# Loading q in 1 KB pieces, four tokens to a partition, in a fused retention and ELU feed-forward kernel

## The chip, the cores and the metric

The kernel runs on one core of one Trainium2 chip. The metric is the device time of one execution in microseconds (us); lower is better. A run of the kernel before stands for the median of three timed runs; the profile is of one further execution.

## The reference, cut to what matters

```python
# q, k, v: (8, 8, 576, 64) float32: batch B, heads H, tokens S, head size D
scores = (1 / sqrt(D)) * q @ k.T                  # per batch and head
gamma  = 1 - 2.0 ** (-5 - arange(H))
Dmat   = where(rel >= 0, gamma ** rel, 0)         # rel = query token - key token
ret    = (scores * Dmat) @ v
x      = ret.transpose(0, 2, 1, 3).reshape(4608, 512)
h      = x @ w_in                                 # w_in: (512, 2048)
g      = where(h > 0, h, exp(min(h, 0)) - 1)
out    = g @ w_out                                # w_out: (2048, 512)
```

The first half is causal retention with one decay for each head, the second a feed-forward layer with an ELU between its two products. Nothing is normalised over a row, so the causal part can be split into blocks with a running state between them.

## The kernel before, in words

**Units.** The first 512 tokens of each batch are cut into four units, 32 in all (`seq`, NS = 32). For the first three batches (units 0 to 11) a unit is 256 tokens (T is 0 or 1) of four heads (w is 0 or 1). From batch 3 on the units are "fine": 128 tokens of all eight heads. The last 64 tokens of each batch are "riders" that are taken along later. The change touches units 0 to 11 alone, and the riders only in the name of a table.

**A unit's steps.** `load(u)` issues three DMAs of 256 KB from SP: q and k into the two halves of the tile rqk, v into rv. In units 0 to 11 a partition holds two neighbouring tokens (e is 0 or 1) of four heads, so the DMA moves pieces of 2 tokens x 64 x 4 bytes = 512 bytes, 128 partitions x 4 heads = 512 pieces to a load. `cast_qk` multiplies q by its decay table gq, k by gk, and rounds to bf16 into the tile qkn, in one instruction for each e; the engine is named by the caller (VectorE "v" or GpSimd "p"). `cast_v` rounds v into vn. `turn_pe` turns q and k on TensorE with eight transposes into PSUM and two copies into qkT (units 0 to 6); `turn` does the same with a transposing DMA from SP (unit 7 on). `scores` makes key x query blocks in the PSUM tile sc, `masks` multiplies by the causal mask into pt, `inter` adds what the running state gives, `values` multiplies pt by v, and `put_x` copies the result to xt, which is x transposed. `state`, `prefix_mid` and `prefix_end` update the running state (mid, end), whose bf16 copies on GpSimd go to s_pair and s_last.

**Feed-forward.** `ffn1` and `ffn1_half` multiply xt by w_in, the ELU runs on ScalarE (exp, relu) and VectorE (one combination), and `ffn2` multiplies by w_out. The weights come as 32 DMAs of 256 KB in 2 KB pieces (`load_w`) and are rounded to bf16 by `cast_w`.

**Order.** Each engine keeps the order in which the program issues (`pin`). By hand it is: loads of units 0 to 3 (unit 3 with v first, then k, then q), twelve weight loads, then units 0 to 3 as they arrive; then the feed-forward of batch 0 beside the remaining weights; the loads of unit 4, four more weight loads, and units 5 to 9 follow on SP. `turn_pe(4)`, `stretch(4)`, `turn_pe(5)`, `stretch(5)` and so on sit between quarters of `ffn2` (`quad`). Unit 7's transposing DMA follows the loads of unit 9 on SP. From there on `stage` mixes feed-forward jobs with one `step` per unit.

**DMA completion.** In the built program every DMA from SP takes the next of eight completion semaphores in turn and waits, before it is issued, for the DMA eight places earlier. The tile rqk has ten buffers, which units and weight loads share.

Of the kernel before, what the change touches and what calls it, by code (L numbers as in the profile page):

```python
# [17 lines left out]
def kernel(  # L18
# [23 lines left out]
    MID = S // 2  # L42
    C = 64
# [3 lines left out]
    const = ctx.enter_context(tc.tile_pool(name="const", bufs=1))  # L47
# [15 lines left out]
    pin = tc.keep_in_program_order  # L63
    def mm(*a, **kw):
        pin(nc.tensor.matmul(*a, **kw))  # L65
# [15 lines left out]
    pos_i = const.tile([P, NU], I32, name="pos_i")  # L81
    nc.gpsimd.iota(pos_i[:, :FT].rearrange("p (t e) -> p t e", e=2), pattern=[[2 * P, 2], [1, 2]], base=-MID,
                   channel_multiplier=2)
    nc.gpsimd.iota(pos_i[:ST, FT:], pattern=[[0, 1]], base=FT * P - MID, channel_multiplier=1)
    nc.gpsimd.iota(pos_i[ST:, FT:], pattern=[[0, 1]], base=MID - FT * P, channel_multiplier=-1)
    pos = const.tile([P, NU], FP32, name="pos")
# [5 lines left out]
    bt = const.tile([P, 1], FP32, name="bt")  # L92
    nc.vector.memset(bt[:ST], math.log(scale))
    nc.vector.memset(bt[ST:], 0.0)
    expo = const.tile([P, NU, H], FP32, name="expo")
    nc.vector.tensor_tensor(
        expo,
        pos.unsqueeze(2).to_broadcast([P, NU, H]),
        lgt.unsqueeze(1).to_broadcast([P, NU, H]),
        ALU.mult,  # L100
    )
    gq = const.tile([P, NU, H], FP32, name="gq")
    nc.scalar.activation(gq[:, :FT], expo[:, :FT], AF.Exp, bias=bq)
    nc.scalar.activation(gq[:, FT], expo[:, FT], AF.Exp, bias=bt)
# [4 lines left out]
    mask = const.tile([P, 2, 2, C], BF16, name="mask")  # L109
    nc.vector.memset(mask, 1.0)  # L110
    for c in range(2):
        for ek in range(2):
            for eq in range(2):
                m = mask[c * C : (c + 1) * C, ek, eq]
                nc.gpsimd.affine_select(out=m, in_=m, compare_op=ALU.is_ge, fill=0.0, base=eq - ek,
                                        pattern=[[2, C]], channel_multiplier=-2)

    mask_t = const.tile([P, ST], BF16, name="mask_t")
    pf_i = const.tile([P, FT], I32, name="pf_i")
# [54 lines left out]
    xps, begun = [None, None], set()  # L174

    def load(u, last=False):
        b, T, w = seq[u]
        rqk = raw.tile([P, 2, 4, 2, D], FP32, name="rqk", tag="rqk")
        rv = raw.tile([P, 4, 2, D], FP32, name="rv", tag="rv", bufs=5)
        parts = [(rqk[:, 0], q), (rqk[:, 1], k), (rv, v)]  # L180
        if fine(u):
            t = u % 4
            for dst, src in parts:
                pin(nc.sync.dma_start(
                    dst.rearrange("p a e d -> p (a e) d"), src[b, :, t * P : (t + 1) * P, :].rearrange("h p d -> p h d"),
                ))
            rawt[u] = rqk, rv
            return
        for dst, src in parts[::-1] if last else parts:
            pin(nc.sync.dma_start(  # L190
                dst.rearrange("p h e d -> p h (e d)"),
                src[b, 4 * w : 4 * w + 4, 2 * P * T : 2 * P * (T + 1), :].rearrange("h (p e) d -> p h (e d)", e=2),
            ))
        rawt[u] = rqk, rv

    def cast_qk(u, i, eng, es=(0, 1)):
        b, T, w = seq[u]
        if fine(u):
            pin(tt[eng](  # L199
                natt[u][0][:, i].rearrange("p e h d -> p (e h) d"), rawt[u][0][:, i].rearrange("p a e d -> p (a e) d"),  # L200
                (gqf, gkf)[i][:, u % 4].unsqueeze(2).to_broadcast([P, H, D]), ALU.mult,
            ))
            return
        x = rawt[u][0][:, i].rearrange("p h e d -> p e h d")
        g = (gq, gk)[i][:, 2 * T : 2 * T + 2, 4 * w : 4 * w + 4].unsqueeze(3).to_broadcast([P, 2, 4, D])
        for e in es:
            pin(tt[eng](natt[u][0][:, i, e], x[:, e], g[:, e], ALU.mult))  # L207

# [58 lines left out]
    def scores(u):  # L267
        sc = ps_s.tile([P, 2, 512], FP32, name="sc", tag="sc")
        if fine(u):

            for m, i, c in fines:
                cs, r = half(c), half(i)
                mm(sc[cs, i, m * C : (m + 1) * C], trt[u][r, HP + m, cs], trt[u][r, m, cs],
                   start=(m == 0), stop=True, skip_group_check=True)
            score_ps[u] = sc
            return
        for hl in range(2):
            for ek in range(2):
                for i in range(2):
                    r = half(i)  # L280
                    for c in range(2):
                        cs = slice(c * C, (c + 1) * C)
                        o = (hl * 2 + ek) * P
                        mm(pairs(sc[cs, i, o : o + P]), trt[u][r, 4 + ek * 2 + hl, cs], queries(u, r, hl, c),
                           start=True, stop=True)
        score_ps[u] = sc

# [25 lines left out]
    def inter(u, hls=(0, 1), to=None):  # L313
        b, T, w = seq[u]
        x = to or xps
        if fine(u):
            for m, i, c in fines:
                if u % 4 + c:
                    r = half(c)
                    q = trt[u][r, m, r] if i == c else swapped[u][r, m]  # L320
                    acc_x(c, i, x[c][half(i), m * C : (m + 1) * C], s_fine[u % 2][r, m, i], q)
            return
        for c in range(2):
            if T + c == 0:
                continue
            s = s_mid[w] if c else s_first[w]
            for hl in hls:
                acc_x(c, 2, pairs(x[c][:, hl * P : (hl + 1) * P]), s[:, hl], queries(u, slice(0, P), hl, c), to)

    def values(u, hls=(0, 1), to=None):  # L330
        vn, pt = natt[u][1], ptt[u]
# [14 lines left out]
    def put_x(u, hls=(0, 1), to=None, eng="ss"):  # L346
        b, T, w = seq[u]
        h0, h1 = hls[0], hls[-1] + 1
        for c in range(2):
            if fine(u):  # L350
                o = w * P + c * C
                pin(engines[eng[c]](xt_tile(b)[:, T, :, o : o + C], xps[c][:, : HP * C].rearrange("p (m n) -> p m n", m=HP)))  # L352
                continue
            src = (to or xps)[c][:, : 2 * P].rearrange("p (h e r) -> p h e r", h=2, e=2)[:, h0:h1]
            dst = xt_tile(b)[:, T, 2 * w + h0 : 2 * w + h1, c * P : (c + 1) * P].rearrange("p h (r e) -> p h e r", e=2)
            pin(engines[eng[c]](dst, src))  # L356

    def drop(u):
# [106 lines left out]
    def cast_rider(b):  # L465
        qkt = nat.tile([P, H, D], BF16, name="qkt", tag="qkt", bufs=2)
        vt = nat.tile([P, HP, D], BF16, name="vt", tag="vt", bufs=2)
        natr[b] = qkt, vt
        rqt, rvt = rawr.pop(b)
        g = gq[:, FT].unsqueeze(2).to_broadcast([P, H, D])  # L470
# [493 lines left out]
```

## Time and profile before

| | |
|---|---|
| median of three timed runs | 303.39 us (303.18 to 303.61) |
| the profiled execution | 303.71 us, of which the span 301.9 us |
| TensorE busy in the span | 293.6 us (97%) |
| ScalarE, VectorE, GpSimd busy | 210.6, 175.3, 175.5 us |
| read from HBM | 36.70 MB |
| DMA packets | 132909, of them 18432 are 512-byte pieces of q, k and v of units 0 to 11 (12 units x 3 x 512) |

The page divides the span into 40 slices and shows for each how busy an engine was. A view of stretches gives the same for chosen times, with the granted TensorE clock, the mean busy share of the 16 DMA engines (their packets overlap, so it can exceed 1) and the rate in GB/s. A timeline row has the start, the duration, the engine, the source line, the operation and its tiles; brackets hold how long the engine had been idle before, and what ended that. The chain of work that ended last is followed back from the last instruction, at each step to what released it.

### The profile page before, as it was taken

How to read it: one execution, taken by the hardware profiler on the slowest of the kernel's cores; microseconds unless marked ns; L12 is line 12 of the kernel's file. 1: busy time of each engine (PE TensorE's matmuls, PEld its weight loads, DVE VectorE, ACT ScalarE, POOL GpSimd, SP SyncE). 2: the span in 40 equal slices, each digit the busy share in tenths (PEclk: the TensorE clock that was granted, in tenths of full speed). 3: DMA queues.
4: the chain of work that ended last, by engine and by line, in shares of the span. 5: the costliest groups of instructions: out<-in, count | busy, mean ns of one | idle time of the engine just before them, and what ended most of it. 6: DMA issues, size and time to landing. Idle time of an engine off the chain costs nothing.

```text
span 301.9 us, 9531 instructions
## 1 busy us (share of the span) xinstructions
PE 293.6 (97%) x3814; PEld 194.6 (64%) x3814; DVE 175.3 (58%) x355; ACT 210.6 (70%) x431; POOL 175.5 (58%) x344
## 2 busy tenths in 40 slices
PE   8889999999999999999999999999999999999995
PEld 5544447776666676666666666666666666666654
DVE  4756567765556756666574367665756575534430
ACT  4779847977776677767676766777776777777651
POOL 5789887777957585858392318585868741311000
PEclk9999999999999999999999999999999999999999
DMA  7999999999999999999976095989999411000112
GB/s 200 313 373 344 347 306 284 227 244 168 247 193 223 187 212 195 211 211 214 208 167 182 35 174 132 186 145 204 201 198 203 107 38 38 37 35 37 57 48 72
DMA packets 132909, 54.37 MB, mean 180 GB/s; under 512 B 107712, under 2 KB 126400, under 8 KB 132864
## 3 DMA queue, kind: packets, MB, share of 16 engines
q1 hardware_dynamic: 130112, 45.04, 74.1%
q0 software_dynamic: 2672, 8.65, 8.3%
q8 instruction: 30, 0.49, 0.7%
q14 instruction: 15, 0.12, 0.1%
q10 hardware_dynamic: 80, 0.07, 0.1%
HBM read 36.70 MB, written 9.44 MB: 153 GB/s over the span
## 4 chain that ended last, share of the span: by engine, by line
PE 82%; DMA 11%; SPq 3%; DVE 1%; issue 0%; ACT 0%; DVEq 0%
PE pm L65 37%; PE ph L65 36%; DMA rqk<-in_moe_w_out_dram 6%; PE x L65 4%; PE sc L65 3%; SPq L190 3%; DMA rqk<-in_q_dram 2%; DMA rqk<-in_moe_w_in_dram 2%; DMA qkT<-qkn 1%; PE pe L65 1%; DVE pt L302 1%; SPq L154 1%; PE ptr L241 0%; DVE qkn L207 0%; ACT oe L931 0%
## 5 line engine op out<-in xcount | busy, mean ns | idle before, releaser
L592 DVE SCALAR_TENSOR_TENSOR g<-e,ph 128x512 bf16<-128x512 f32 x128 | 87.6, 687 | 91.2 <-ACT ph L591 82.4
L65 PEld LDWEIGHTS <-w_in_sb 128*128 128x128 bf16 x1088 | 105.2, 98 | 43.1 <-issue 0.7
L65 PE MATMUL ph<-xt,w_in_sb 128*128 128x256 bf16 (+1 forms) x960 | 131.5, 280 | 0.7 <-ACT xt L356 0.4
L65 PE MATMUL pm<-w_out_sb,g 128*128 128x512 bf16 x512 | 131.9, 379 | 0.0
L588 ACT ACTIVATE e<-ph 128x512 f32<-128x512 f32 x144 | 86.0, 597 | 58.8 <-PE ph L65 58.6
L591 ACT ACTIVATE ph<-ph 128x512 f32<-128x512 f32 x144 | 85.7, 595 | 0.0
L65 PEld LDWEIGHTS <-g 128*128 128x128 bf16 x512 | 48.7, 98 | 35.4 <-issue 0.3
L417 POOL CAST s_fine<-run 64x256 bf16<-64x256 f32 x40 | 15.9, 397 | 52.2 <-DVE run L389 39.6
L645 POOL DMA_DIRECT2D out_dram<-ot x35 | 20.0, 572 | 33.4 <-ACT ot L635 33.4
L635 ACT COPY ot<-pm 128x512 f32<-128x512 f32 x35 | 20.5, 588 | 9.1 <-PE pm L65 9.0
L199 POOL TENSOR_TENSOR qkn<-rqk,gqf 128x512 bf16<-128x512 f32 x20 | 21.1, 1055 | 0.4
L199 POOL TENSOR_TENSOR qkn<-rqk,gkf 128x512 bf16<-128x512 f32 x20 | 21.0, 1048 | 0.0
L592 DVE SCALAR_TENSOR_TENSOR gt<-e,ph 128x512 bf16<-128x512 f32 x16 | 11.0, 686 | 13.8 <-ACT ph L591 12.7
L352 ACT CAST xt<-x 128x256 bf16<-128x256 f32 x40 | 12.9, 377 | 5.7 <-PE x L65 5.7
L65 PE MATMUL ph<-xtail,w_in_sb 128*128 128x256 bf16 x128 | 16.6, 273 | 0.0
L207 POOL TENSOR_TENSOR qkn<-rqk,gk 128x256 bf16<-128x256 f32 x24 | 14.2, 614 | 3.9 <-DMA rqk<-in_k_dram 3.6
L389 DVE TENSOR_TENSOR run<-sc,run 128x256 f32<-128x256 f32 x35 | 14.9, 424 | 1.2
L210 POOL CAST vn<-rv 128x512 bf16<-128x512 f32 x23 | 14.0, 610 | 1.4
L295 DVE TENSOR_TENSOR pt<-sc,mask_t 128x512 bf16<-128x512 f32 x20 | 13.7, 683 | 0.0
L423 POOL CAST s_fine<-run 64x256 bf16<-64x256 f32 x30 | 11.9, 396 | 1.8
L437 POOL CAST s_pair<-mid 64x128 bf16<-64x128 f32 x24 | 6.9, 288 | 10.3 <-DVE mid L389 5.0
L302 DVE TENSOR_TENSOR pt<-sc,mask 128x1024 bf16<-128x1024 f32 x10 | 12.2, 1219 | 0.7 <-PE sc L65 0.5
(92 smaller groups left out, 261.8 us busy)
## 6 DMA issues: line engine op xcount, KB each, us to landing
rqk<-in_q_dram SPq DMA_DIRECT2D x32, 256.0 KB, 4.7
rqk<-in_k_dram SPq DMA_DIRECT2D x32, 256.0 KB, 5.3
rv<-in_v_dram SPq DMA_DIRECT2D x32, 256.0 KB, 5.6
out_dram<-ot POOLq DMA_DIRECT2D x31, 256.0 KB, 3.9
rqk<-in_moe_w_in_dram SPq DMA_DIRECT2D x16, 256.0 KB, 5.5
rqk<-in_moe_w_out_dram SPq DMA_DIRECT2D x16, 256.0 KB, 5.8
rqt<-in_q_dram SPq DMA_DIRECT2D x8, 128.0 KB, 5.5
rqt<-in_k_dram SPq DMA_DIRECT2D x8, 128.0 KB, 4.9
```

What stands on the lines that cost most here:

```text
L65: pin(nc.tensor.matmul(*a, **kw))
L199: pin(tt[eng](natt[u][0][:, i].rearrange("p e h d -> p (e h) d"), rawt[u][0][:, i].rearrange("p a e d -> p (a e) d"), (gqf, gkf)[i][:, u % ...
L207: pin(tt[eng](natt[u][0][:, i, e], x[:, e], g[:, e], ALU.mult))
L210: pin(engines[eng](natt[u][1], rawt[u][1]))
L302: pin(nc.vector.tensor_tensor(ptt[u].rearrange("p i h n -> p (i h) n"), sc.rearrange("p i (h n) -> p (i h) n", h=2), m.to_broadcast([P, 4, ...
L389: pin(nc.vector.tensor_tensor(dst, a, b, ALU.add))
L417: pin(nc.gpsimd.tensor_copy(s_fine[u % 2][half(1), :, i], new[half(i), 0]))
L588: pin(nc.scalar.activation(e, ph, AF.Exp))
L591: pin(nc.scalar.activation(ph, ph, AF.Relu))
L592: pin(nc.vector.scalar_tensor_tensor(dst, view(e), -1.0, view(ph), ALU.add, ALU.min))
L635: pin(nc.scalar.copy(ot, pm))
L645: pin((queue or nc.gpsimd).dma_start(dst, src))
```

## The change

q of units 0 to 11 is laid out otherwise: a partition holds four neighbouring tokens of two heads, partitions 0 to 63 the heads 0 and 1 of the four, partitions 64 to 127 the heads 2 and 3. q's load becomes two DMAs of 128 KB in pieces of 1 KB, each into 64 partitions. k and v stay as they were. The decay table for q is made anew in this layout (gq from expq), the rider's table gets a tile of its own (gt); the mask, `queries`, `inter`, `scores` and `put_x` follow the order of the tokens (four runs of 32 where there were two of 64). The q cast becomes one instruction of 128 x 512, other than in unit 3, where it stays in two.

```diff
+    NQ = 8
+    pos_i = const.tile([P, NQ + NU], I32, name="pos_i")
+    for hl in range(2):
+        nc.gpsimd.iota(pos_i[hl * C : (hl + 1) * C, :NQ]..., channel_multiplier=4)
...
+    lgq = const.tile([P, 2, 2], FP32, name="lgq")          # two copies of 64 x 4
+    expq = const.tile([P, NQ, 4], FP32, name="expq")       # one product of 128 x 32
+    gq = const.tile([P, 2, 4, 2, 2], FP32, name="gq")
+    nc.scalar.activation(gq.rearrange("p t e w i -> p (t e) (w i)"), expq, AF.Exp, bias=bq)
...
+    mask = const.tile([P, 2, 4, C // 2], BF16, name="mask")  # 4 affine_selects of 64 x 128, were 8 of 64 x 64
...
         for dst, src in parts[::-1] if last else parts:
+            if src is q:
+                for hl in range(2):
+                    h = 4 * w + 2 * hl
+                    pin(nc.sync.dma_start(
+                        dst[half(hl)].rearrange("p (i a) e d -> p i (a e d)", i=2),
+                        q[b, h : h + 2, 2 * P * T : 2 * P * (T + 1), :].rearrange("i (p e) d -> p i (e d)", e=4),
+                    ))
+                continue
...
+        if i == 0:
+            x = rawt[u][0][:, 0].rearrange("p (i a) e d -> p (a e) i d", i=2)
+            y = natt[u][0][:, 0].rearrange("p e (a i) d -> p (e a) i d", i=2)
+            g = gq[:, T, :, w].unsqueeze(3).to_broadcast([P, 4, 2, D])
+            if es == (0, 1):
+                pin(tt[eng](y, x, g, ALU.mult))
+            else:
+                for e in es:
+                    e = slice(2 * e, 2 * e + 2)
+                    pin(tt[eng](y[:, e], x[:, e], g[:, e], ALU.mult))
+            return
...
     def queries(u, rows, hl, c):
-        return trt[u].rearrange("p (i h) n -> p i h n", h=2)[rows, 0:2, hl, c * C : (c + 1) * C]
+        o = hl * C + c * C // 2
+        return trt[u][rows, :4, o : o + C // 2]
...
-            dst = xt_tile(b)[...].rearrange("p h (r e) -> p h e r", e=2)
+            dst = xt_tile(b)[...].rearrange("p h (r e) -> p h e r", e=4)
```

More of the change, by code (lines that the diff above doesn't have):

```diff
@@ L80 @@
         nc.vector.memset(lgt[:, h : h + 1], lg[h])
-    pos_i = const.tile([P, NU], I32, name="pos_i")
-    nc.gpsimd.iota(pos_i[:, :FT].rearrange("p (t e) -> p t e", e=2), pattern=[[2 * P, 2], [1, 2]], base=-MID,
+    NQ = 8
+    pos_i = const.tile([P, NQ + NU], I32, name="pos_i")
+    for hl in range(2):
+        nc.gpsimd.iota(pos_i[hl * C : (hl + 1) * C, :NQ].rearrange("p (t e) -> p t e", e=4), pattern=[[2 * P, 2], [1, 4]],
+                       base=-MID, channel_multiplier=4)
+    nc.gpsimd.iota(pos_i[:, NQ : NQ + FT].rearrange("p (t e) -> p t e", e=2), pattern=[[2 * P, 2], [1, 2]], base=-MID,
                    channel_multiplier=2)
-    nc.gpsimd.iota(pos_i[:ST, FT:], pattern=[[0, 1]], base=FT * P - MID, channel_multiplier=1)
-    nc.gpsimd.iota(pos_i[ST:, FT:], pattern=[[0, 1]], base=MID - FT * P, channel_multiplier=-1)
-    pos = const.tile([P, NU], FP32, name="pos")
+    nc.gpsimd.iota(pos_i[:ST, NQ + FT :], pattern=[[0, 1]], base=FT * P - MID, channel_multiplier=1)
+    nc.gpsimd.iota(pos_i[ST:, NQ + FT :], pattern=[[0, 1]], base=MID - FT * P, channel_multiplier=-1)
+    pos = const.tile([P, NQ + NU], FP32, name="pos")
     nc.vector.tensor_copy(pos, pos_i)
@@ L94 @@
     nc.vector.memset(bt[ST:], 0.0)
+    lgq = const.tile([P, 2, 2], FP32, name="lgq")
+    for hl in range(2):
+        r = slice(hl * C, (hl + 1) * C)
+        nc.vector.tensor_copy(lgq[r], lgt[r].rearrange("p (w h i) -> p w h i", h=2, i=2)[:, :, hl])
+    expq = const.tile([P, NQ, 4], FP32, name="expq")
+    nc.vector.tensor_tensor(
+        expq,
+        pos[:, :NQ].unsqueeze(2).to_broadcast([P, NQ, 4]),
+        lgq.rearrange("p w i -> p (w i)").unsqueeze(1).to_broadcast([P, NQ, 4]),
+        ALU.mult,
+    )
+    gq = const.tile([P, 2, 4, 2, 2], FP32, name="gq")
+    nc.scalar.activation(gq.rearrange("p t e w i -> p (t e) (w i)"), expq, AF.Exp, bias=bq)
     expo = const.tile([P, NU, H], FP32, name="expo")
@@ L97 @@
         expo,
-        pos.unsqueeze(2).to_broadcast([P, NU, H]),
+        pos[:, NQ:].unsqueeze(2).to_broadcast([P, NU, H]),
         lgt.unsqueeze(1).to_broadcast([P, NU, H]),
@@ L101 @@
     )
-    gq = const.tile([P, NU, H], FP32, name="gq")
-    nc.scalar.activation(gq[:, :FT], expo[:, :FT], AF.Exp, bias=bq)
-    nc.scalar.activation(gq[:, FT], expo[:, FT], AF.Exp, bias=bt)
     gk = const.tile([P, FT, H], FP32, name="gk")
     nc.scalar.activation(gk, expo[:, :FT], AF.Exp, bias=bk, scale=-1.0)
-    mask = const.tile([P, 2, 2, C], BF16, name="mask")
+    gt = const.tile([P, H], FP32, name="gt")
+    nc.scalar.activation(gt, expo[:, FT], AF.Exp, bias=bt)
+    mask = const.tile([P, 2, 4, C // 2], BF16, name="mask")
     nc.vector.memset(mask, 1.0)
@@ L112 @@
         for ek in range(2):
[L113 to L116, printed above, removed]
+            m = mask[c * C : (c + 1) * C, ek]
+            nc.gpsimd.affine_select(out=m, in_=m, compare_op=ALU.is_ge, fill=0.0, base=-ek,
+                                    pattern=[[1, 4], [4, C // 2]], channel_multiplier=-2)
     mask_t = const.tile([P, ST], BF16, name="mask_t")
@@ L189, in load @@
         for dst, src in parts[::-1] if last else parts:
+            if src is q:
+                for hl in range(2):
+                    h = 4 * w + 2 * hl
[4 more added lines that the diff above has]
+                continue
             pin(nc.sync.dma_start(
@@ L244, in queries, with fours @@
     def queries(u, rows, hl, c):
-        return trt[u].rearrange("p (i h) n -> p i h n", h=2)[rows, 0:2, hl, c * C : (c + 1) * C]
+        o = hl * C + c * C // 2
+        return trt[u][rows, :4, o : o + C // 2]
+    def fours(ap):
+        return ap.rearrange("p (e r) -> p e r", e=4)
     def pairs(ap):
@@ L283, in scores @@
                         o = (hl * 2 + ek) * P
-                        mm(pairs(sc[cs, i, o : o + P]), trt[u][r, 4 + ek * 2 + hl, cs], queries(u, r, hl, c),
+                        mm(fours(sc[cs, i, o : o + P]), trt[u][r, 4 + ek * 2 + hl, cs], queries(u, r, hl, c),
                            start=True, stop=True)
@@ L327, in inter @@
             for hl in hls:
-                acc_x(c, 2, pairs(x[c][:, hl * P : (hl + 1) * P]), s[:, hl], queries(u, slice(0, P), hl, c), to)
+                acc_x(c, 2, fours(x[c][:, hl * P : (hl + 1) * P]), s[:, hl], queries(u, slice(0, P), hl, c), to)
     def values(u, hls=(0, 1), to=None):
@@ L353, in put_x @@
                 continue
-            src = (to or xps)[c][:, : 2 * P].rearrange("p (h e r) -> p h e r", h=2, e=2)[:, h0:h1]
-            dst = xt_tile(b)[:, T, 2 * w + h0 : 2 * w + h1, c * P : (c + 1) * P].rearrange("p h (r e) -> p h e r", e=2)
+            src = (to or xps)[c][:, : 2 * P].rearrange("p (h e r) -> p h e r", h=2, e=4)[:, h0:h1]
+            dst = xt_tile(b)[:, T, 2 * w + h0 : 2 * w + h1, c * P : (c + 1) * P].rearrange("p h (r e) -> p h e r", e=4)
             pin(engines[eng[c]](dst, src))
@@ L469, in cast_rider @@
         rqt, rvt = rawr.pop(b)
-        g = gq[:, FT].unsqueeze(2).to_broadcast([P, H, D])
+        g = gt.unsqueeze(2).to_broadcast([P, H, D])
         for hs in (slice(0, H // 2), slice(H // 2, H)):
```

2 lines of the change are left out of this document (1 added, 1 removed).

## The prediction

> **What bounds the kernel now.** I read the page's slices first, then the stretches of the first 60 us, the chain that ended last, TensorE's waits, and the timeline where they pointed.
>
> ```profile
> PE 293.6 (97%) x3814; PEld 194.6 (64%) x3814; DVE 175.3 (58%) x355; ACT 210.6 (70%) x431; POOL 175.5 (58%) x344
> ...
> DMA  7999999999999999999976095989999411000112
> ```
>
> TensorE is busy for 97% of the span, so over most of it only TensorE's own work counts. The DMA engines are full too, from the first slice on, but what TensorE waits for tells where that matters. Its whole list of waits has eight rows, and one alone names a DMA, once:
>
> ```profile
> PE sc L65 <- DMA qkT<-qkn: 0.3, 1, 0.3
> ```
>
> In the timeline there are three places where loads set the pace:
>
> ```profile
> 13.72 1.18 POOL L207 TENSOR_TENSOR qkn<-rqk,gk 128x256 bf16<-128x256 f32 x2 [0.59 <-DMA rqk<-in_k_dram]
> ...
> 14.86 0.84 POOL L207 TENSOR_TENSOR qkn<-rqk,gq 128x256 bf16<-128x256 f32 x1
> ...
> 19.98 3.63 PE L65 MATMUL ph<-xt,w_in_sb 128*128 128x512 bf16 x16 [0.19 <-DVE xt L356]
> ...
> 41.78 0.86 DVE L207 TENSOR_TENSOR qkn<-rqk,gq 128x256 bf16<-128x256 f32 x2 [1.59 <-DMA rqk<-in_q_dram]
> ...
> 44.45 0.61 PE L241 MATMUL ptr<-ident,qkn 128*128 128x128 bf16 x8 [0.66 <-DVE end L389]
> ...
> 55.14 0.42 PE L65 MATMUL sc<-qkT 64*64 64x128 bf16 x16 [0.33 <-DMA qkT<-qkn]
> ```
>
> First, unit 3's k arrives at 13.72; its cast, the cast of half of q behind it on GpSimd, the transposes, scores and the copy to xt lead to 19.98, from where TensorE runs without a gap. Second, VectorE stands 1.59 us for unit 5's q, and behind that cast in its queue are unit 4's mask, mid and end, for which TensorE waits 0.66 at 44.45. Third, unit 7's scores wait 0.33 for a transposing DMA that lies behind all loads to unit 9. The chain shows the second and third as transfers queued for long:
>
> ```profile
> 34.91 6.85 DMA rqk<-in_q_dram
> ...
> 50.81 4.28 DMA qkT<-qkn
> ```
>
> After 55.14 no row of TensorE's waits names a load: whatever shift stands there is carried to the end. So up to 55 us the question is how long the loads take, in their order; behind it, nothing.
>
> **What one q load costs.** The stretches (time, TensorE, weight load, VectorE, ScalarE, GpSimd, clock, DMA share, GB/s) give the rates:
>
> ```profile
> 10.00:12.00 2.00, 1.95 (x60) 1.33 (x58) 1.84 (x3) 1.45 (x4) 1.82 (x5) 1.00 1.17 291
> 24.00:26.00 2.00, 2.00 (x11) 0.88 (x9) 1.37 (x3) 2.00 (x6) 1.87 (x4) 1.00 0.86 291
> 26.00:28.00 2.00, 2.00 (x10) 0.86 (x9) 1.12 (x3) 1.63 (x5) 1.76 (x4) 1.00 1.05 392
> 46.00:48.00 2.00, 2.00 (x62) 1.49 (x62) 1.49 (x4) 1.44 (x4) 1.19 (x3) 1.00 1.17 291
> ```
>
> 512-byte pieces (10 to 12 and 46 to 48) run at 291 GB/s: 262144 bytes in 0.90 us. Weights in 2 KB pieces (26 to 28) run at 392: 0.67 us. The number of pieces falls from 512 to 128 for 0.23 us, 0.60 ns each; with 256 pieces a q load would take 0.67 + 128 x 0.60 = 0.75 us. That is the gain sought: 0.15 us for each of twelve loads. It holds if a load into 64 partitions is as fast as one into 128. No such load with 1 KB pieces is in this trace; two kinds of transfer have half the partitions. The last stores are one tile of 256 KB from 128 partitions, and one in two halves of 128 KB from 64 partitions, both in 2 KB pieces. The DMA view of 292.8 to 293.8 (slices of 25 ns), then that of 296.5 to 298.1 (40 ns):
>
> ```profile
> GB/s 0 82 410 82 328 573 328 328 655 246 164 410 573 246 328 655 246 410 328 573 164 328 573 328 328 655 246 246 246 247 82 82 0 0 0 0 0 0 0 0
> ```
>
> ```profile
> GB/s 0 0 51 307 51 256 154 461 102 154 154 256 307 102 102 307 256 102 51 52 358 103 256 154 461 102 154 154 410 102 154 205 256 205 103 51 103 0 0 0
> ```
>
> The whole tile fills 31 slices of 25 ns, 0.78 us or 338 GB/s; the two halves fill 35 of 40 ns, 1.40 us or 187 GB/s. Nothing else runs, and the bytes and pieces are the same. The other kind are the riders' loads, 64 partitions in 256-byte pieces, issued two upon two just as q would be:
>
> ```profile
> 71.00:72.40 1.40, 1.40 (x13) 0.99 (x11) 1.40 (x2) 0.58 (x3) 0.27 (x1) 1.00 1.39 218
> 79.90:80.60 0.70, 0.70 (x5) 0.32 (x4) 0.30 (x1) 0.52 (x2) 0.69 (x1) 1.00 1.41 180
> ```
>
> A busy stretch of 256-byte pieces into 128 partitions has 218 GB/s, the stretch of a rider's halves 180. So the bounds: 0.75 us without a price for halves, 256 KB / 180 = 1.46 us with the whole of it. The rider row is nearest in direction and in the queue, but its pieces are a quarter as long; the stores have long pieces and show almost a factor of two (338 / 187 = 1.8), which on 0.75 gives 1.35. I take 1.2 us, between them and towards the half-partition rows: +0.30 us for each q load; ends -0.15 and +0.55.
>
> [...]
>
> **The sum.** Loads go through one queue in order, and the queue stays full.
> - *Unit 3's k (13.72)* has the q of units 0, 1 and 2 before it: 3 x 0.30 = +0.9. The cast of q behind it on GpSimd starts at 14.86 + 0.9 = 15.76. Unit 3's q, whose load ends 4 x 0.30 = 1.2 later, landed no later than 14.86 before, so it is there by 16.0 at worst; I count +0.9 for the start at 19.98.
> - *Unit 5's q (41.78)* has six q loads up to and with itself: +1.8. Part of it is taken up between: in the stretch 24 to 26 the DMA share is 0.86 against 1.05 after it, 2 x 0.19 / 1.05 = 0.35 us not used, which a late queue would fill. That leaves +1.45. The cast behind it becomes one instruction (below), -0.17. TensorE is itself 0.9 later, so its stall of 0.66 grows by 0.4 and its lateness is 1.3.
> - *Unit 7's transposing DMA (55.14)* has ten q loads before it: 3.0 - 0.35 = +2.65. TensorE comes 1.3 later, so the stall of 0.33 grows by 1.35. Sum: **+2.65 us**.
> - The q loads of units 10 and 11 come behind; no later scores wait for a DMA, so they are hidden, up to the slack of those units, which the trace gives no size for.
>
> **The other edits.**
>
> ```profile
> L207 DVE TENSOR_TENSOR qkn<-rqk,gq 128x256 bf16<-128x256 f32 x13 | 5.3, 448 | 3.8 <-DMA rqk<-in_q_dram 3.8
> ...
> L308 DVE TENSOR_TENSOR pt<-sc,mask 128x512 bf16<-128x512 f32 x4 | 2.7, 688 | 1.7 <-PE sc L65 1.7
> ...
> L356 ACT CAST xt<-x 128x256 bf16<-128x256 f32 x22 | 8.3, 451 | 3.3 <-PE x L65 3.0
> ...
> L352 ACT CAST xt<-x 128x256 bf16<-128x256 f32 x40 | 12.9, 377 | 5.7 <-PE x L65 5.7
> ```
>
> The q cast on VectorE, two of 128 x 256 that took 0.86 together at 41.78, becomes one of 128 x 512 at about 0.69 (by the mask row of that size): -0.17, counted above at unit 5 alone. The first unit's transposes now wait for the whole cast, not for a half, which ends at about the same time. `put_x` writes with a step of four elements instead of two: the rows of the copy with a step of two (451) and with none (377) bound it at 0 to 0.07 us each, and ScalarE has 30% free. `scores` and `inter` have as many instructions of the same size, reading four runs of 32 columns: 0. The tables get two iotas, two copies and a product more:
>
> ```profile
> 1.68 0.13 POOL L85 IOTA pos_i<- 64x1 int32 x1
> ...
> 3.69 0.76 DVE L207 TENSOR_TENSOR qkn<-rqk,gq 128x256 bf16<-128x256 f32 x2 [1.12 <-DMA rqk<-in_q_dram]
> ```
>
> Two iotas of 0.13 to 0.2 and three small VectorE instructions of 0.1 to 0.2 lie in the 1.12 us in which VectorE waits for the first q: hidden. On SP each unit issues one DMA more:
>
> ```profile
> L154 SPq DMA_DIRECT2D rqk<-in_moe_w_out_dram x16: 327/328/856, 15.5 to 34.2; - x16
> ...
> L190 SPq DMA_DIRECT2D rqk<-in_q_dram x12: 379/745/1319, 0.8 to 56.1; - x12
> ```
>
> An issue costs 0.33 to 0.38 us where nothing holds it. Behind it on SP are k, v and the next unit; SP runs up to 6.85 us ahead of the landing, which covers it, so 0. Were that cover gone, it would be 10 x 0.35 = 3.5 us. The eight completion semaphores now hold two units (1.5 MB, 5 us at 291 GB/s) instead of 2 MB; the first q, issued at 0.8 into an empty queue, is being cast at 3.69, so 5 us still cover a load's way.
>
> The profiled execution (303.71, span 301.9) would become 306.4; on the median of 303.39, which is 0.32 lower, **306.0 us**.
>
> **The rivals.**
> - *Halves cost nothing* (other side). Two halves follow each other in the queue, and if the engines drift apart, one half's end overlaps the other's start. The q load takes 0.75. Then unit 3's k is 0.45 earlier; unit 5's q is 0.9 earlier with a cast 0.17 shorter, so 0.62 of the 0.66 goes; the 0.33 goes too: -1.4, 302.0 us. For it speaks 392 against 291 GB/s; against it both half-partition rows. It decides where a q load takes under 0.90.
> - *Price and gain cancel.* With the riders' ratio, 218 / 180 = 1.21, the load takes 0.75 x 1.21 = 0.91; only the shorter cast remains, -0.2: 303.2 us. It needs the price to be as small for long pieces as for short ones, which the stores deny.
>
> **How the numbers follow.** Forecast 0.68, halves free 0.20, cancel 0.12. A measurement of this kernel tells about 0.2% (0.6 us) from no change. Within the forecast, +0.10 to +0.55 a load gives +0.65 (10 x 0.10 - 0.35) to +5.15 us, 304.0 to 308.5. The range 302.6 to 307.8 leaves out most of the free case and the forecast's top. Faster: 0.20 and a little of the cancelling case, 0.21. Same: the rest of that case, 0.09. Slower: 0.70.
>
> **What would show it.** In the profile after: a stretch with q loads among 512-byte loads below 291 GB/s; unit 3's k cast at about 14.6; the start now at 19.98 at about 20.9; TensorE's wait of 0.66 at 1.0 to 1.1, that of 0.33 at about 1.7. If q loads take 0.75, those starts come earlier and both waits shrink. I am wrong if the q loads are slow and yet the stalls do not grow, that is if the queue had slack that I counted as full, or if a new wait appears after 60 us.

## The result

The changed kernel takes 312.22 us (median of six runs, 309.46 to 314.57), the kernel before 303.63 in the same session (303.18 to 304.18): 8.6 us more, ratio 1.0249 [1.0208, 1.029] with its 95% interval. The ratio is of the fast runs alone: the one of 314.57, over 1.5% above the quickest, is left out of it, and the median of the other five is 311.33. The forecast was 306.0, +2.6 against its 303.39; the sign holds, the size doesn't. The profiled execution is the quickest of the six (309.46, span 307.8), so its trace shows 5.75 of the 8.6 us; where in time the rest lies is read from other kernels' traces below.

Of the page of the changed kernel, the rows that stood for the kernel before, and the granted clock:

```profile
PE 296.6 (96%) x3814; PEld 195.5 (64%) x3814; DVE 175.9 (57%) x352; ACT 216.3 (70%) x431; POOL 174.7 (57%) x337
...
PEclk9977999999999999999999999999999999999998
DMA  6999999999999999999998166989899611000112
```

TensorE is busy for 3 us more and still idle for 4% of the span; its clock falls to 0.7 in the third and fourth slice, 15 to 31 us. Its waits, longest in total first (total, times, longest):

```profile
PE ptr L276 <- POOL qkn L242: 1.2, 4, 0.4
PE ph L65 <- ACT xt L395: 1.2, 2, 0.9
PE x L65 <- DVE lgt L80: 1.1, 1, 1.1
PE ptr L276 <- DVE qkn L233: 1.0, 1, 1.0
PE sc L65 <- DMA qkT<-qkn: 0.8, 2, 0.6
```

The places of the prediction in the timeline, the start of the chain in front of them, and the chain at unit 7:

```profile
4.53 0.69 DVE L233 TENSOR_TENSOR qkn<-rqk,gq 128x512 bf16<-128x512 f32 x1 [1.14 <-DMA rqk<-in_q_dram]
...
15.22 1.18 POOL L242 TENSOR_TENSOR qkn<-rqk,gk 128x256 bf16<-128x256 f32 x2 [1.20 <-DMA rqk<-in_k_dram]
16.92 0.86 POOL L237 TENSOR_TENSOR qkn<-rqk,gq 128x256 bf16<-128x256 f32 x1 [0.52 <-DMA rqk<-in_q_dram]
20.20 1.01 PE L65 MATMUL ph<-xt,w_in_sb 128*128 128x512 bf16 x2 [0.93 <-ACT xt L395]
22.81 5.65 PE L65 MATMUL ph<-xt,w_in_sb 128*128 128x512 bf16 x17
48.47 0.61 PE L276 MATMUL ptr<-ident,qkn 128*128 128x128 bf16 x8
59.78 0.42 PE L65 MATMUL sc<-qkT 64*64 64x128 bf16 x16 [0.57 <-DMA qkT<-qkn]
74.89 0.42 PE L65 MATMUL sc<-qkT 64*64 64x128 bf16 x16 [0.24 <-DMA qkT<-qkn]
```

```profile
10.73 6.05 DMA rqk<-in_q_dram
...
54.91 4.83 DMA qkT<-qkn
```

The first q cast starts 0.84 us later than before (3.69), unit 3's k cast 1.50 later (13.72), and the cast of half of its q on GpSimd 2.06 later (14.86), now waiting for the load, which the chain names too. The unbroken run of the dense feed-forward starts 2.83 later (19.98), and its matmuls run at half the clock (0.50 granted from 20 to 26 us): 17 take 5.65 us where 16 took 3.63. At unit 5's transposes the wait of 0.66 is gone, since TensorE itself comes 4.02 later; at unit 7's scores the wait is 0.57 and the lateness 4.64. The transposing DMA in front of them is issued at 54.91, behind casts that are late with TensorE, but it lands 1.0 us behind unit 9's v (58.74 and 59.74 in the trace), so its place in the queue sets the time. Another 1.2 us come behind that, one row of it a DMA's (0.24 at 74.89). The stretches (time, busy time of TensorE, weight load, VectorE, ScalarE and GpSimd, clock, DMA share, GB/s), first of before, then of after:

```profile
2.00:4.00 2.00, 2.00 (x11) 1.31 (x9) 0.85 (x4) 0.81 (x4) 1.47 (x8) 1.00 0.94 277
46.00:48.00 2.00, 2.00 (x62) 1.49 (x62) 1.49 (x4) 1.44 (x4) 1.19 (x3) 1.00 1.17 291
48.00:50.00 2.00, 2.00 (x59) 1.27 (x57) 1.85 (x5) 1.25 (x3) 1.76 (x5) 1.00 1.17 294
```

```profile
2.00:4.00 2.00, 2.00 (x11) 1.32 (x9) 1.27 (x5) 0.77 (x4) 1.38 (x6) 1.00 0.54 164
20.00:22.00 2.00, 1.79 (x13) 0.53 (x12) 1.24 (x3) 0.74 (x3) 2.00 (x4) 0.50 1.04 380
46.00:48.00 2.00, 2.00 (x40) 1.13 (x40) 1.42 (x2) 0.00 (x0) 0.52 (x1) 1.00 1.18 241
48.00:50.00 2.00, 2.00 (x21) 1.05 (x18) 1.32 (x3) 1.70 (x4) 1.69 (x5) 1.00 1.16 228
```

From 46 to 50 us both kernels load q, k and v of whole units, and the DMA engines are equally busy (1.17), yet they move 234.5 GB/s instead of 292.5. A unit of 786432 bytes takes 3.35 us instead of 2.69. k and v are loaded as before, so I put the whole +0.66 to the q load, where the forecast had +0.30. Last, the copy of x to xt, and SP's issues of q:

```profile
L395 ACT CAST xt<-x 128x256 bf16<-128x256 f32 x22 | 14.4, 789 | 3.9 <-PE x L65 3.8
```

```profile
L209 SPq DMA_DIRECT2D rqk<-in_q_dram x24: 595/606/1824, 0.8 to 62.1; - x24
```

The copy takes 789 ns where it took 451: +0.34 us each, where the prediction had 0 to 0.07. And one issue takes at least 0.60 us, not 0.33 to 0.38.

### The profile page after: what moved, and what is told of

Its sections match the earlier page's. It is cut to its first block, busy times and chain, and to the rows that moved or that the text cites. A ratio compares the mean times of both kernels' runs of the same rounds, so it can differ in the third digit from the quotient of the medians.

```text
span 307.8 us, 9542 instructions
## 1 busy us (share of the span) xinstructions
PE 296.6 (96%) x3814; PEld 195.5 (64%) x3814; DVE 175.9 (57%) x352; ACT 216.3 (70%) x431; POOL 174.7 (57%) x337
## 4 chain that ended last, share of the span: by engine, by line
PE 85%; DMA 6%; SPq 3%; ACT 2%; POOL 1%; DVE 1%; issue 1%; POOLq 0%; ACTq 0%
PE ph L65 38%; PE pm L65 38%; DMA qkT<-qkn 4%; PE x L65 4%; PE sc L65 3%; DMA rqk<-in_q_dram 2%; SPq L209 2%; SPq L214 1%; PE pe L65 1%; ACT xt L395 1%; PE ptr L276 1%; PE st L65 1%; DVE pt L341 0%; POOL qkn L242 0%; POOL qkn L233 0%
## 5 line engine op out<-in xcount | busy, mean ns | idle before, releaser
L65 PE MATMUL ph<-xt,w_in_sb 128*128 128x256 bf16 (+1 forms) x960 | 134.1, 282 | 1.6 <-ACT xt L395 1.2
L456 POOL CAST s_fine<-run 64x256 bf16<-64x256 f32 x40 | 15.9, 398 | 52.5 <-DVE run L428 39.2
L242 POOL TENSOR_TENSOR qkn<-rqk,gk 128x256 bf16<-128x256 f32 x24 | 15.0, 643 | 5.4 <-DMA rqk<-in_k_dram 5.3
L395 ACT CAST xt<-x 128x256 bf16<-128x256 f32 x22 | 14.4, 789 | 3.9 <-PE x L65 3.8
L391 ACT CAST xt<-x 128x256 bf16<-128x256 f32 x40 | 12.9, 377 | 5.4 <-PE x L65 5.4
```

What stands on the lines that cost most here:

```text
L456: pin(nc.gpsimd.tensor_copy(s_fine[u % 2][half(1), :, i], new[half(i), 0]))
```

## The experiments

Theory: the lateness is queue time of the q loads, and it comes from the partitions that one DMA reaches. Rivals: the second DMA and its issue, the copy with a step of four, and the half clock at the start. The kernel before was measured beside each group, with medians of 303.98 to 304.62. In halves_only, full_1k, put4_only, changed_put2, halves_step2, halves_first4 and halves_rest the rows of q or of x lie in another order than the computation takes them to lie, so they compute something else with the same instructions and sizes. Seven kernels came out above the range that the theory gave them: halves_only (by 1.5 us), halves_512 (1.1), changed_warm (0.7), changed_parity (0.6), halves_step2, halves_rest and two_full (0.1 to 0.4; 303 to 305 us was the range for halves_step2); none of the seven lies in a rival's range.

| kernel | median us | ratio to before |
|---|---|---|
| halves_only | 311.49 | 1.0212 [1.0171, 1.0253] |
| full_1k | 303.40 | 0.9963 [0.9938, 0.9989] |
| put4_only | 305.83 | 1.0031 [1.0002, 1.0059] |
| changed_put2 | 312.11 | 1.0249 [1.0206, 1.0291] |
| halves_512 | 314.10 | 1.0327 [1.0286, 1.0369] |
| halves_step2 | 305.35 | 1.0053 [1.0029, 1.0077] |
| two_full | 305.14 | 1.0023 [1.0004, 1.0042] |
| halves_first4 | 306.26 | 1.0076 [1.0046, 1.0106] |
| halves_rest | 309.48 | 1.0166 [1.0114, 1.0218] |
| changed_parity | 307.06 | 1.0097 [1.0068, 1.0125] |
| changed_warm | 313.24 | 1.0288 [1.0243, 1.0332] |
| changed_put_read | 311.65 | 1.0253 [1.0189, 1.0317] |
| changed_by_head | 358.78 | 1.1781 [1.1755, 1.1807] |
| by_head_put_read | 358.14 | 1.1767 [1.174, 1.1794] |
| before_put_read | 304.29 | 0.9999 [0.9979, 1.0018] |
| parity_put_read | 305.81 | 1.0069 [1.0047, 1.0092] |

### The changed load and the changed copy, each alone

**halves_only**: the kernel before with the changed q loads.

```diff
+            if src is q:
+                for hl in range(2):
+                    h = 4 * w + 2 * hl
+                    pin(nc.sync.dma_start(
+                        dst[half(hl)].rearrange("p (i a) e d -> p i (a e d)", i=2),
+                        q[b, h : h + 2, 2 * P * T : 2 * P * (T + 1), :].rearrange("i (p e) d -> p i (e d)", e=4),
+                    ))
+                continue
```

> The kernel before with the changed q loads alone: two DMAs of 128 KB, 1 KB pieces, 64 partitions each; casts, tables, order of tokens and copies as before, so q's tokens are not where the computation takes them to be. Theory 'loads' (the halves and their issue make the time): most of the lateness comes back, 307 to 310 us, the first q cast at about 4.5 us, stretches with q, k and v loads at 225 to 240 GB/s. Rival 'copy' (the copies of x with a step of four elements, 789 ns against 451, make it): at most 304.5 us.

**full_1k**: 1 KB pieces into all 128 partitions with one DMA (512 tokens of two heads, other rows of q than the unit's).

```diff
+            if src is q:
+                h = 4 * w + 2 * T
+                pin(nc.sync.dma_start(
+                    dst.rearrange("p (i a) e d -> p i (a e d)", i=2),
+                    q[b, h : h + 2, : 4 * P, :].rearrange("i (p e) d -> p i (e d)", e=4),
+                ))
+                continue
```

> The kernel before with q in 1 KB pieces in one DMA into all 128 partitions (two heads of 512 tokens for each unit, so q's data are other tokens than the computation takes them to be). Theory 'halves' (64 partitions are the price, not the length of the pieces): a q load at 330 to 350 GB/s, 0.75 to 0.80 us, the kernel 0 to 1.4 us faster than before, 302.2 to 303.4. Rival 'length or count of pieces': loads slow here too, 305 us or more.

**put4_only**: the kernel before with the copy's step of four; its edit is shown. **changed_put2**: the changed kernel with the step of two, the same edit the other way round.

```diff
-            src = ....rearrange("p (h e r) -> p h e r", h=2, e=2)[:, h0:h1]
-            dst = ....rearrange("p h (r e) -> p h e r", e=2)
+            src = ....rearrange("p (h e r) -> p h e r", h=2, e=4)[:, h0:h1]
+            dst = ....rearrange("p h (r e) -> p h e r", e=4)
```

> The kernel before with the copy of x in the changed order alone (step of four elements instead of two in the destination; the rows of a token block land in another order). Theory 'copy': 0.34 us more for each of 22 copies, of which those of units 0 to 2 and of unit 3's halves lie on the way to the feed-forward: 1 to 2.5 us, 304.5 to 306. Theory 'loads': the copies are hidden but for the last, below 304.0.

> The changed kernel with the copy of x in the order of before (step of two; the rows of a token block land in another order). Theory 'loads': 1 us or less off the changed kernel. Theory 'copy': 2 us or more off. Both together: the time that remains over before is that of halves_only within 0.7 us. If the granted clock of the first 30 us stays at 1.00, the clock's part shows as what is gained beyond the copies' own 0.34 us each.

The loads alone cost 6.87 us, 2.1 of the 2.5%. The copy alone costs 1.2 by the medians, 0.3% by the ratio, whose interval begins at 1.0002; 305.83 lies where the theory 'copy' had it, so in this kernel the copy is not hidden. Taken out of the changed kernel it brings nothing: there the loads are later than the copy, and in the trace of changed_put2 TensorE waits 2.07 at unit 5's transposes and 2.64 at unit 7's scores. halves_only shows the forecast's own mechanism, larger. Its TensorE waits in the timeline:

```profile
20.89 3.63 PE L65 MATMUL ph<-xt,w_in_sb 128*128 128x512 bf16 x16 [0.18 <-DVE xt L364]
...
47.90 0.81 PE L249 MATMUL ptr<-ident,qkn 128*128 128x128 bf16 x8 [2.44 <-DVE end L397]
...
60.94 0.42 PE L65 MATMUL sc<-qkT 64*64 64x128 bf16 x16 [1.08 <-DMA qkT<-qkn]
```

The start comes at 20.89, as forecast for the loads (20.9). That is in part luck: halves_first4, whose loads are the same up to there, starts at 22.04, and three loads at +0.66 make 2.0 us, not 0.9. Then VectorE's queue stands for unit 5's q and TensorE waits 2.44 (forecast 1.0 to 1.1), and unit 7's scores come 5.80 us later than in the kernel before. With full_1k the time falls by 0.4%, and the stretches show pieces of 1 KB at work:

```profile
46.00:48.00 2.00, 1.84 (x61) 1.49 (x61) 1.51 (x3) 1.48 (x4) 1.19 (x3) 1.00 1.14 310
48.00:50.00 2.00, 1.85 (x58) 1.27 (x57) 1.83 (x5) 1.21 (x3) 1.76 (x5) 1.00 1.14 310
```

At 310 GB/s a unit takes 2.54 us, 0.15 less than in the kernel before: the gain that the prediction worked out from the weights (0.90 - 0.75). The longer pieces do what they were to do.

### Which property of the load

**halves_step2** writes the even and the odd partitions instead of the lower and the upper 64; **two_full** issues two DMAs of two heads into all partitions, in 512-byte pieces; **halves_512** keeps the two halves, but in 512-byte pieces (128 tokens of four heads to a half).

```diff
# halves_step2, otherwise as halves_only
+                        dst[hl::2].rearrange("p (i a) e d -> p i (a e d)", i=2),
# two_full
+                        dst[:, 2 * hl : 2 * hl + 2].rearrange("p h e d -> p h (e d)"),
+                        q[b, h : h + 2, 2 * P * T : 2 * P * (T + 1), :].rearrange("h (p e) d -> p h (e d)", e=2),
# halves_512, t = 2 * P * T + P * hl
+                        dst[half(hl)].rearrange("p h e d -> p h (e d)"),
+                        q[b, 4 * w : 4 * w + 4, t : t + P, :].rearrange("h (p e) d -> p h (e d)", e=2),
```

> As halves_only (q loads of the kernel before as two DMAs of 128 KB in 1 KB pieces, 64 partitions each, q's data not where the computation takes them to be), but one DMA takes the even partitions, the other the odd ones, instead of 0 to 63 and 64 to 127. [...] Rival 'two DMAs' (their number and issue): as halves_only, 310 us or more.

> The kernel before with each q load as two DMAs of 128 KB into all 128 partitions (two heads each, 512-byte pieces); results and everything else as before. Theory 'which partitions': 303.5 to 305 us, the issue on SP costs 0.3 to 0.5 us more for a unit and delays the first q little. Rival 'two DMAs': 308 us or more.

> The kernel before with each q load as two DMAs of 128 KB, partitions 0 to 63 and 64 to 127, with the 512-byte pieces of before; results and everything else as before. Theory 'which partitions': slower like halves_only or a little more, 309 to 313 us. Rival 'length' (only long pieces suffer in a half): 304 to 306 us.

The same stretches, of halves_512 and of halves_step2:

```profile
46.00:48.00 2.00, 1.95 (x40) 1.10 (x40) 1.80 (x3) 0.00 (x0) 1.35 (x5) 1.00 1.15 222
48.00:50.00 2.00, 1.60 (x14) 0.87 (x13) 1.39 (x5) 1.50 (x3) 1.67 (x5) 1.00 1.15 227
```

```profile
46.00:48.00 2.00, 1.54 (x14) 0.88 (x13) 1.39 (x6) 1.56 (x4) 1.84 (x6) 1.00 1.01 283
48.00:50.00 2.00, 1.84 (x56) 1.27 (x56) 1.62 (x4) 1.86 (x5) 1.44 (x3) 1.00 0.98 296
```

halves_512 moves 224.5 GB/s: 3.50 us for a unit, +0.81 over the 2.69 of the same pieces in 128 partitions. With 1 KB pieces the halves cost the same 0.81 (3.35 - 2.54). halves_step2 differs from halves_only in the partitions of each DMA alone, and has 289.5 GB/s, with DMA engines not quite full (1.01 and 0.98), and a ratio of 1.0053 instead of 1.0212. So the price, 0.81 us for a q load, belongs to loads that reach only the partitions 0 to 63 or only 64 to 127, not to 64 partitions as such, to the second DMA (two_full, +0.2%) or to the pieces. Why such loads cost more, no run here shows.

### Where the loads count

**halves_first4** has the load of halves_only in units 0 to 3 only, **halves_rest** in units 4 to 11 only.

```diff
-            if src is q:
+            if src is q and u < 4:      # halves_first4
+            if src is q and u >= 4:     # halves_rest
```

> As halves_only, but only in units 0 to 3; units 4 to 11 load q as before. If the lateness is that of the whole queue up to unit 7's transposing DMA, a third of halves_only's remains: 305.5 to 307.5 us, of it about 1 us at the start of the feed-forward. If the first four units make all of it (late start, clock at half speed): 309 us or more. If they make nothing: 304.5.

> The kernel before, with the changed q loads alone (two DMAs into partitions 0 to 63 and 64 to 127, 1 KB pieces) in units 4 to 11; units 0 to 3 load q as before, casts and scores are as before, so the rows of q in those units are other tokens. Theory (each such load costs queue time, and the cost of the loads adds up until the queue empties): the same loads in all twelve units cost 6.9 us, in units 0 to 3 alone 2.0 us; here the rest, +4 to +5 us, 308.2 to 309.3 on a kernel before of 304.3; TensorE's wait for VectorE at unit 5's q and its wait for a transposing DMA stay about as long as with all twelve. Rival (the harm is done at the start, where the four first units hold up the dense feed-forward and its clock): +1 us or less, under 305.5.

+2.04 and +4.99 us make 7.03, and all twelve cost 6.87: the loads add up, as queue time does, within the noise (the interval of halves_rest is 1.6 us to either side), and the start alone does not make the loss.

**changed_warm** keeps the clock up at the start of the changed kernel: from 18 to 26 us it is 1.00 throughout, where the changed kernel has 0.84 and, from 20 us on, 0.50. It has more of the matmuls whose results are not used (`warm`): 12 instead of 7 at the start, 6 within unit 3's turn, 4 ahead of the dense feed-forward.

```diff
-    warm(7)
+    warm(12)
-    turn_pe(3, "vs", order=(1, 0))
+    turn_pe(3, "vs", between=6, order=(1, 0))
+    warm(4, banks[1][1])
```

> The changed kernel with more of the matmuls that only keep TensorE's clock up: 12 instead of 7 at the start, 6 between the steps of unit 3's turn, 4 ahead of the first dense part. Nothing else differs. Theory (the loads are late until 55 us, so time won earlier is lost again at unit 5's q and at unit 7's transposing DMA): the clock between 18 and 26 us comes back, the start moves by at most 1 us, the whole by less than 1 us, 311.2 to 312.5. Rival (the half clock from 19.7 to 26.5 us is a cost that is carried to the end): 2 to 3 us less, 309 to 310.

```profile
22.88 4.07 PE L65 MATMUL ph<-xt,w_in_sb 128*128 128x512 bf16 x17
...
48.85 0.61 PE L276 MATMUL ptr<-ident,qkn 128*128 128x128 bf16 x8 [1.88 <-DVE end L428]
...
62.59 0.42 PE L65 MATMUL sc<-qkT 64*64 64x128 bf16 x16 [2.89 <-DMA qkT<-qkn]
...
73.72 0.42 PE L65 MATMUL sc<-qkT 64*64 64x128 bf16 x16
```

```profile
64.00:66.00 2.00, 2.00 (x9) 1.14 (x8) 0.82 (x3) 1.69 (x4) 1.16 (x5) 0.50 1.15 268
```

Unit 8's scores in the kernel before:

```profile
64.48 0.42 PE L65 MATMUL sc<-qkT 64*64 64x128 bf16 x16
```

The 17 matmuls take 4.07 us instead of 5.65, and it is all given back: TensorE waits 1.88 at unit 5's transposes and 2.89 at unit 7's scores, and the whole is no faster. The half clock at the start is not what the change costs; TensorE can be early or late at 27 us, the queue sets 60. But the half clock returns behind the long wait: it is 0.50 from 64 to 66 us, and unit 8's scores, which wait for nothing, come at 73.72, 9.24 later than in the kernel before (64.48), where unit 7's were 7.45 later. These 1.8 us are in no term of the prediction. I read them as a cost of the wait, which no kernel here shows by itself, and changed_warm is no test of the kernel without a half clock. In changed_put2 the clock stays at 1.00 behind its wait of 2.64, and the lateness stays too: 8.00 at unit 7's scores (63.14), 7.97 at unit 8's (72.45). A wait need not end that way, then; what decides it was not tried.

The trace of changed_warm took 313.41 us, and unit 7's scores are 2.81 later in it than in the changed kernel's profiled execution, which took 309.46. The trace of changed_put_read (below; the same loads, 314.58 us) has them at 62.97, the clock at 0.50 behind them and unit 8's scores at 75.17, 10.69 late. That the longer executions of the changed kernel itself lose their time in the same two places is likely; no trace of them was taken.

### The whole change with other loads and another copy

**changed_parity**: the changed kernel with even and odd partitions; the decay table of q, the positions and the columns of `queries` follow.

```diff
-                        dst[half(hl)].rearrange("p (i a) e d -> p i (a e d)", i=2),
+                        dst[hl::2].rearrange("p (i a) e d -> p i (a e d)", i=2),
...
-        o = hl * C + c * C // 2
-        return trt[u][rows, :4, o : o + C // 2]
+        return trt[u][rows, :4, c * C + hl : (c + 1) * C : 2]
```

> The changed kernel whole, but a q load's two DMAs write the even and the odd partitions instead of 0 to 63 and 64 to 127; tables and the columns that the queries are read from follow. Pieces (1 KB), number of DMAs, the copy with a step of four and the casts are as in the changed kernel. Theory (which partitions a DMA reaches is the cost): +0.3 to +0.7 per cent over the kernel before, 305.2 to 306.5, with unit 3's k cast back at 13.5 to 14.3 and 44 to 54 us back at 255 GB/s or more. Rival (64 partitions at a time, wherever they lie, or another edit of the change): 310 or more.

**changed_put_read**: the changed kernel with the copy walked in the order of the tokens, so that the step is in what is read.

```diff
-            src = ....rearrange("p (h e r) -> p h e r", h=2, e=4)[:, h0:h1]
-            dst = ....rearrange("p h (r e) -> p h e r", e=4)
+            src = ....rearrange("p (h e r) -> p h r e", h=2, e=4)[:, h0:h1]
+            dst = ....rearrange("p h (r e) -> p h r e", e=4)
```

> The changed kernel with put_x's copy walked in the order of the tokens: it writes runs without a step and reads the accumulator with the step of 64 columns instead. Nothing else differs. Theory (the 789 ns of the copy are the price of writing with a step of four two-byte elements, and in the whole kernel the late loads cover it): the copy's mean falls to 400 to 560 ns and the time by less than 1 us, 311.3 to 312.5. Rival (the longer copy is a cost of its own in the changed kernel): 0.9 us or more less, under 311.3. If the copy stays near 789, the order of writing is not what it pays for.

The copy of changed_put_read, beside 789 ns in the changed kernel:

```profile
L395 ACT CAST xt<-x 128x256 bf16<-128x256 f32 x22 | 7.1, 377 | 7.6 <-PE x L65 7.5
```

377 ns is the row of a copy without any step: the price is in the step of writing, and the step of reading is free here. In the changed kernel that brings nothing (1.0253 against 1.0249). Even and odd partitions bring 1.0249 down to 1.0097, above the +0.3 to +0.7% expected. **parity_put_read** has both edits, **before_put_read** the copy's alone in the kernel before.

> The changed kernel whole with both remedies: a q load's two DMAs write the even and the odd partitions, and put_x's copy is walked in the order of the tokens. Theory (with the loads nearly on time the copy's 0.4 us for each call is no longer covered and costs about what the step of four cost in the kernel before, 0.9 us): ratio to the kernel before 1.005 to 1.008, against 1.0097 with the copy's step of four. Rival (the copy is hidden here as in the changed kernel, and all of the 1.0 per cent belongs to the divided load): 1.009 or more.

> The kernel before with put_x's copy alone walked in the order of the tokens: 377 ns instead of 451. Theory (where the loads set the pace up to 55 us the copy costs nothing unless it is much longer): within 0.3 us of the kernel before, ratio 0.999 to 1.001. Rival (each us of the copy ahead of the dense feed-forward counts): 0.2 us or more less, in proportion to the +0.9 us that the step of four cost there, 0.9 * 74 / 347 = 0.2.

parity_put_read comes out at 1.0069, in the range of the theory, but the intervals of it and of changed_parity overlap, so a part of the copy is not shown. In the kernel before 378 ns instead of 451 bring nothing. What is left, 0.7%, is near halves_step2's 0.5%: two issues for each load and a first q that comes later (SP's issue again 602 ns at least). It was not divided further.

**changed_by_head** divides the load the other way, one head of either half into all 128 partitions; **by_head_put_read** has the copy in the order of the tokens as well.

```diff
+                for i in range(2):
+                    h = 4 * w + i
+                    pin(nc.sync.dma_start(
+                        dst[:, 2 * i : 2 * i + 2].rearrange("p a e d -> p (a e d)"),
+                        q[b, h : h + 3 : 2, 2 * P * T : 2 * P * (T + 1), :].rearrange("hl (p e) d -> hl p (e d)", e=4),
+                    ))
```

> The changed kernel whole, with its two DMAs of a q load divided the other way: each takes one head of either half into all 128 partitions, in one piece of 1 KB to a partition. The layout in the buffer, the number of DMAs and the length of the pieces are those of the changed kernel. Theory (the partitions that one DMA reaches are the cost, and pieces of 1 KB into 128 are a little faster than of 512 bytes): the loss of 8 us goes but for the second issue and the copy with a step of four, +0.9 at most: 303.8 to 305.5 on a kernel before of 304.4, with 264 GB/s or more in 44 to 54 us. Rival (two DMAs of 128 KB upon one buffer, or another edit of the change): 307 or more.

> The same with put_x's copy walked in the order of the tokens, as in changed_put_read. Theory (with the loads on time the copy is no longer covered, and its 789 ns against 451 cost about 0.9 us, as in the kernel before): 0.6 to 1.2 us less than changed_by_head, 302.8 to 304.5, the same as the kernel before or up to 0.5 per cent faster. Rival (the copy's price is hidden here too): as changed_by_head, within 0.3 us.

Both miss by over 50 us. The stretches of changed_by_head:

```profile
2.00:4.00 2.00, 2.00 (x11) 1.32 (x9) 1.23 (x5) 0.81 (x4) 1.33 (x6) 1.00 0.09 17
...
10.00:12.00 2.00, 1.28 (x9) 1.04 (x10) 1.16 (x3) 0.00 (x0) 1.14 (x3) 0.50 0.14 40
```

While only q is under way (10 to 12 us) the 16 DMA engines are busy to 0.14 on the mean and move 40 GB/s. The source's outermost dimension is the two heads here, where in the changed kernel it is the 64 groups of four tokens; whether that is the cause was not tried. With so few bytes moved, for whatever reason, these two kernels tell nothing of the partitions or of the copy.

## Why the prediction was wrong

**The step that failed: "I take 1.2 us, between them and towards the half-partition rows: +0.30 us for each q load."** A q load costs +0.66, above the upper end of +0.55: -0.15 for the pieces, as forecast, and +0.81 for the halves. 0.81 on a load of 0.90 is a factor of 1.9, on 0.75 one of 2.1. The store rows had shown 1.8, with long pieces and nothing beside them; the value chosen, 1.2, was 1.6 times 0.75, moved towards the riders' 1.21. No run shows a q load of 1.2 us; in the changed kernel it takes 1.56 (0.90 + 0.66). With 0.66 the prediction's own sum gives 10 x 0.66 - 0.35 = +6.25 at unit 7's scores; the traces have +4.64, +5.80 (halves_only) and +7.45 (changed_warm) there. The measured +8.6 lies above +6.25 as well: what the half clock adds behind unit 7 (1.8 in changed_warm) is in no term of the sum, and why the queue is later in one execution than in another stays open.

**Mechanism and places: right up to 60 us.** The queue is full up to unit 7's transposing DMA (a DMA share of 1.11 to 1.20 from 40 to 54 us in the changed kernel); taken alone, the loads move the start to 20.89 and then hold TensorE at unit 5 and at unit 7, and the loads of the first four and the other units add up. The rates below 291 GB/s show it. The stalls did not grow as listed in the changed kernel's own trace (0.66 gone, 0.33 to 0.57 instead of 1.7), since TensorE was late already, by 4.02 at unit 5: the split of the lateness over the places was wrong. "After 55.14 no row of TensorE's waits names a load: whatever shift stands there is carried to the end" no longer holds with a later queue: a wait of 0.24 stands at 74.89, and the shift can grow by the half clock (1.8 us in changed_warm, as I read it). The prediction had named both, stalls that do not grow and a new wait after 60 us, as signs of being wrong.

**"0 to 0.07 us each" for `put_x`: wrong,** +0.34. A step of two (451) and none (377) do not bound a step of four. put4_only puts its price at 0.3% of the time where loads are punctual; in the changed kernel it is covered.

**"SP runs up to 6.85 us ahead ... so 0": wrong at the start.** There SP has no lead, an issue costs 0.60, and the DMA engines stand at 0.54 in 2 to 4 us where they had 0.94. two_full, whose q issues take 0.38 us at least, prices the second issue at 0.2%. In halves_step2 they take 0.60 as here, and all that it adds to the kernel before is 0.5%.

**The rivals.** "Halves cost nothing" and "price and gain cancel" both fall with halves_only; what the first describes is full_1k (-0.4%), and halves_step2 (+0.5%) is the nearest to the second.

## What to carry to other kernels

A transfer that is divided over partitions should be divided so that each part still spans both 0 to 63 and 64 to 127 (even and odd, say): the ratio was 1.0053 in halves_step2 against 1.0212 in halves_only. Nor should it be divided as in changed_by_head, with the two heads outermost, which ran at 40 GB/s here. Longer pieces pay only after that: a unit took 2.54 us with them in one DMA for q, 3.35 with them in halves, and 2.69 without them. Where a trace holds a row that shows the disputed property with nothing else beside it (here the stores, 1.8), take that row and do not average it with one from another regime. A saving ahead of a full queue is worth nothing until the queue is shorter: neither the copy nor the clock at the start bought anything while the loads were late (1.0249 in changed_put2 and 1.0288 in changed_warm against 1.0249). And the clock may fall behind a long wait: in changed_warm it was 0.50 behind one of 2.89 us, and the lateness grew by a further 1.8 us; in changed_put2 it stayed at 1.00 behind one of 2.64.

## What was not expected of the hardware

- Two loads into partitions 0 to 63 and 64 to 127 cost about twice one into 128 (+0.81 on 0.90 us) with 512-byte and with 1 KB pieces; into even and odd partitions at most 0.18 more than one load of the same 1 KB pieces (2.72 us for a unit at 289.5 GB/s against 2.54).
- ScalarE's copy of 128 x 256 to bf16: 377 ns without a step, 451 with a step of two in what is written, 789 with four, and 377 when the step is in what is read from PSUM.
- Behind waits of 2.44 us (halves_only) and 2.89 us (changed_warm) TensorE's clock stood at 0.54 (48 to 50 us) and 0.50 (64 to 66 us); behind one of 2.64 us (changed_put2) it stayed at 1.00.
- Loads of two heads with the heads outermost (changed_by_head, 10 to 12 us) moved 40 GB/s, with the 16 DMA engines busy to 0.14.
- No kernel here is faster than the kernel before and computes the same: full_1k is faster, but its units would have to be 512 tokens of two heads, which was not tried.
